# Part of the last gate's weights loaded early, on GpSimd's DMA queue, onto chosen partitions

## The chip, the cores and the metric

One core of a Trainium2 chip runs one decode step of a transformer block for four sequences. The metric is device time in microseconds (us), the median of several runs. The core has five engines with a queue each: TensorE (PE, whose weight loads the profile lists as PEld), VectorE (DVE), ScalarE (ACT), GpSimd (POOL) and SyncE (SP). All loads from HBM go through 16 DMA engines, which the queues of SP, ACT and GpSimd feed.

## What is computed

The reference, cut to what matters:

```python
mod = (silu(c) @ w_mod).reshape(4, 6, 1, -1)          # c: 4x512, w_mod: 512x3072
sa, ca, ga, sb, cb, gb = (mod[:, i] for i in range(6))
h = layernorm(x) * (1 + ca) + sa
x = x + ga * attention(h, last 2048 keys and values of 8192, wq, wo)
h = layernorm(x) * (1 + cb) + sb
x = x + gb * ((silu(h @ w1) * (h @ w3)) @ w2)          # w1, w3: 512x1792, w2: 1792x512
```

The last gate, gb, is `silu(c)` (4x512) times the last 512 columns of `w_mod`: 512 weight rows of 512 numbers, 1 MiB in float32. Keys, values and weights together are 101.2 MB, and nothing is read twice.

## The kernel before

Everything is float32. The sequence of loads is written out by hand on SP's queue (`load`, L88 to L125), in the order in which the data are used: the tile `T0` with `c` and two parts of `w_mod`, then for each of eight key/value heads 8 MB into one of two big buffers `KV[0]`, `KV[1]`, with the attention weights `wq`, `wo` (tile `WP`) between them, then the weights of the other gates (`wm_in`), of w1 and w3 (`f1_in`, `f2_in`), of gb (`gb_in`, L123), and at last w2 in six pieces (`W2_CUTS`, L124 and L125). ACT's queue takes the first `WP` load and x. SP waits before a load until the buffer's last reader is done (`x_done`, `a_done`, `qt_done`), and otherwise issues ahead. GpSimd only fills a few tiles at the start (L128 to L139) and passes semaphores on.

`sc` (L188) is silu(c), transposed: 128 partitions by 4 chunks by 4 sequences. PE forms the first modulations from it at the start (L303), and SP's load of the second head waits for them (L95). After the attention loop come, on PE: the modulations ga, sb, cb (L381, into bank bX), the transposes of the normalized h (L405), the products with w1 and w3 (L416 to L432), the transposes of u (L447), the gate gb (L454: four matmuls, one for each chunk of 128 weight rows, into four bands of 32 partitions of bank bM, that a later product with `same` adds up, L474), and the products with w2 (L462 to L485), each piece after its own load. VectorE multiplies by the gate (L488), adds x (L490), and SP stores the result (L492).

Matmuls are recorded in the helper `mm`, so in the profile all of them have its line, L255; loads by SP have L89 and transposes in `turn` L276.

Of the kernel before, what the change touches and what calls it, by code (L numbers as in the profile page):

```python
# [5 lines left out]
AF = mybir.ActivationFunctionType  # L6
# [4 lines left out]
B, D, HQ, G, SK, DH, W, FF = 4, 512, 32, 8, 8192, 128, 2048, 1792  # L11
P = 128
# [2 lines left out]
EPS = 1e-5  # L15
CHUNKS = [(j, c) for c in range(4) for j in range(4) if c < 2 or j < 3]
HEAD = 8
W2_CUTS = [0, 4, 8, 10, 12, 13, 14]
PAIRS = G // 2

# [20 lines left out]
        return (self.sem, self.n)  # L41


def block_kernel(nc, x_in, t0_in, t1_in, kv_in, w_in, wm_in, f1_in, f2_in, gb_in, w2_in, out):
    T, v, s, gp, S = nc.tensor, nc.vector, nc.scalar, nc.gpsimd, nc.sync

    def sems(names):
        return [nc.alloc_semaphore(n) for n in names.split()]

    def sb(name, cols, rows=P):  # L50
        return nc.alloc_sbuf_tensor(name, (rows, cols), F32).ap()

    def bank(name):
        return nc.alloc_psum_tensor(name, (P, 512), F32).ap()

    (first,) = sems("first")
    A = Queue(nc, s, "act")
    V = Queue(nc, v, "dve")
    L = Queue(nc, gp, "pool")
    dx, dt0, dt1, dkv, dk, dva, dvb, dwo, dm, df1, df2a, df2b, dgb = sems("dx dt0 dt1 dkv dk dva dvb dwo dm df1 df2a df2b dgb")  # L60
    dw = sems(" ".join(f"dw{i}" for i in range(len(W2_CUTS) - 1)))
    z_ok, q_ok, p_ok, k_ok, va_ok, vb_ok, pt_ok, o_ok, ot_ok = sems("z_ok q_ok p_ok k_ok va_ok vb_ok pt_ok o_ok ot_ok")
    s_done, q_done, qt_done, pp_done, o_done, x_done, a_done, pe, last = sems("s_done q_done qt_done pp_done o_done x_done a_done pe last")
# [1 line left out]

    KV = [sb("KV0", 16384), sb("KV1", 16384)]
    WP = sb("WP", 8192)
    T0 = KV[1][:, : 16 + 4096]
    x_sb = sb("x_sb", 512, B)
    ident, same, eps = sb("ident", P), sb("same", B), sb("eps", 1)  # L70
    sc, e1, e2 = sb("sc", 16), sb("e1", 16), sb("e2", 16)
    hT, h2T = sb("hT", 16), sb("h2T", 16)
    Z = sb("Z", B * 28)
    q_sb, p_sb, o_sb, a_sb, y_sb, g_sb, u_sb, gb_sb = [sb(n, 512) for n in "q_sb p_sb o_sb a_sb y_sb g_sb u_sb gb_sb".split()]
# [10 lines left out]
    bS, bQ, bT, bP, bO, bX, bA, bM = [bank(n) for n in "bS bQ bT bP bO bX bA bM".split()]  # L85


    def load(dst, src, sem):  # L88
        S.dma_start(dst, src).then_inc(sem, 16)  # L89

    load(T0, t0_in, dt0)
    s.dma_start(WP[:, 4096:], t1_in).then_inc(dt1, 16)
# [27 lines left out]
    S.wait_ge(x_done, G)  # L120
    load(KV[1][:, :3072], f2_in[:, :3072], df2a)
    load(KV[1][:, 3072:6144], f2_in[:, 3072:], df2b)
    load(KV[1][:, 6144:8192], gb_in, dgb)  # L123
    for a, b, sem in zip(W2_CUTS[:-1], W2_CUTS[1:], dw):  # L124
        load(KV[1][:, 8192 + a * 512 : 8192 + b * 512], w2_in[:, a * 512 : b * 512], sem)  # L125


    l_eps = L.op(gp.memset(eps, EPS))  # L128
    t = L.op(gp.memset(ident, 0.0))
    L.wait(t)  # L130
# [48 lines left out]
    v_same = V.op(v.tensor_reduce(same, ident.rearrange("p (j i) -> p i j", i=32)[:, :B, :], axis=AX.X, op=ALU.add))  # L179

    A.wait((dt0, 16))
    t = A.op(s.activation(e1, T0[:, :16], AF.Exp, scale=-1.0))
    V.wait(t)
    t = V.op(v.tensor_scalar(e2, e1, 1.0, None, op0=ALU.add))
    V.wait(t)
    t = V.op(v.reciprocal(e2, e2))
    V.wait(t, (dt0, 16))
    t_sc = V.op(v.tensor_mul(sc, T0[:, :16], e2))  # L188

    A.wait((pe, 1))  # L190
    t_sa = A.op(s.copy(sa_sb, bM[32 : 32 + B, :]))
# [1 line left out]
    t = V.op(v.scalar_tensor_tensor(xs, bM[:B, :], 1.0, xc, op0=ALU.add, op1=ALU.mult))  # L193
# [60 lines left out]
    def mm(o, lhsT, rhs, start=True, stop=True):  # L254
        return T.matmul(o, lhsT, rhs, start=start, stop=stop, skip_group_check=True)  # L255
# [46 lines left out]
    T.wait_ge(V.sem, t_sc[1])  # L302
    for k in range(4):  # L303
        for i in range(2):
            ins = mm(bM[32 * i : 32 * i + B, :], sc[:, k * B : (k + 1) * B], T0[:, 16 + (2 * k + i) * 512 : 16 + (2 * k + i + 1) * 512], k == 0, k == 3)
    ins.then_inc(pe, 1)
    T.wait_ge(V.sem, t_h[1])
    for k in range(4):
        ins = T.transpose(bT[:, k * B : (k + 1) * B], h[:, k * P : (k + 1) * P], ident[:B, :B])
# [71 lines left out]
    for k in range(4):  # L381
        for i in range(3):
            at = (3 * k + i) * 512
            ins = mm(bX[32 * i : 32 * i + B, :], sc[:, k * B : (k + 1) * B], KV[0][:, at : at + 512], k == 0, k == 3)
# [3 lines left out]

    V.wait((pe, 3), t_ga)
    t = V.op(v.tensor_mul(ag, bM[:B, :], ga_sb))  # L390
    V.wait(t)
    t_x1 = V.op(v.scalar_tensor_tensor(x1, ag, 1.0, x_sb, op0=ALU.mult, op1=ALU.add, accum_out=st2[:, 0:1]))
    t_ss, t_r0, t_xc = stats(x1, t_x1, st2)
# [10 lines left out]
    for k in range(4):  # L404
        ins = T.transpose(bT[:, k * B : (k + 1) * B], h[:, k * P : (k + 1) * P], ident[:B, :B])  # L405
# [4 lines left out]
    def view(t_):  # L410
        return t_.rearrange("p (c j i) -> p c j i", c=4, j=4)
# [4 lines left out]
    for k in range(4):  # L416
        for j in range(4):
            at = 6144 + k * 2048 + j * 512
            ins = mm(bQ[32 * j : 32 * j + B, :], h2T[:, k * B : (k + 1) * B], KV[0][:, at : at + 512], k == 0, k == 3)
# [3 lines left out]
    for k in range(4):  # L423
# [5 lines left out]
        for j in range(3):  # L429
            at = k * 1536 + j * 512  # L430
            ins = mm(bA[32 * j : 32 * j + B, :], h2T[:, k * B : (k + 1) * B], KV[1][:, at : at + 512], k == 0, k == 3)
    ins.then_inc(pe, 1)  # L432
    A.wait((pe, 7))
    t = A.op(s.activation(view(eT), view(bP)[:, :, :, :B], AF.Exp, scale=-1.0))
    V.wait(t)
    t = V.op(v.tensor_scalar(dT, eT, 1.0, None, op0=ALU.add))
    V.wait(t)
    t = V.op(v.reciprocal(rT, dT))
# [7 lines left out]
    for c in range(4):  # L446
        ins = T.transpose(bS[:, c * P : c * P + 96], u_sb[:96, c * P : (c + 1) * P], ident[:96, :96])  # L447
# [3 lines left out]


    T.wait_ge(dgb, 16)
    for k in range(4):  # L454
        ins = mm(bM[32 * k : 32 * k + B, :], sc[:, k * B : (k + 1) * B], KV[1][:, 6144 + 512 * k : 6144 + 512 * (k + 1)])
    ins.then_inc(pe, 1)
    A.wait((pe, 10))
    t_gb = A.op(s.copy(gb_sb, bM))
    T.wait_ge(V.sem, t_hid[1])
    hw = view(hidT)  # L460
    w2 = KV[1][:, 8192 : 8192 + 14 * 512].rearrange("p (n m) -> p n m", n=14)
    for i in range(len(W2_CUTS) - 1):  # L462
        T.wait_ge(dw[i], 16)
        for n in range(W2_CUTS[i], W2_CUTS[i + 1]):
            jj, c = CHUNKS[n]
            if n < HEAD:
                ins = mm(bO[32 * (n % 4) : 32 * (n % 4) + B, :], hw[:, c, jj, :], w2[:, n, :], n < 4, n >= HEAD - 4)
                continue
            for j in range(4):
                ins = mm(bX[32 * j : 32 * j + B, :P], hw[:, c, jj, :], w2[:, n, j * P : (j + 1) * P], n == HEAD, n == 13)  # L470
        if i == 0:
            T.wait_ge(A.sem, t_gb[1])
            for j in range(4):
                ins = mm(bT[32 * j : 32 * j + B, :P], same, gb_sb[:, j * P : (j + 1) * P])  # L474
# [13 lines left out]
    t = V.op(v.tensor_mul(yt, bX[:, :P], gbJ))  # L488
# [8 lines left out]
def _layout(i):  # L497
    import numpy as np

    def a(t):  # L500
        return np.ascontiguousarray(t)

    k = i["A_k_cache"][:, :, SK - W :, :].reshape(B, G, NT, 512, DH)
    v = i["A_v_cache"][:, :, SK - W :, :].reshape(B, G, NT, 4, P, DH)
    k = k.transpose(1, 4, 2, 0, 3).reshape(G, P, 8192)
    v = v.transpose(1, 4, 2, 0, 3, 5).reshape(G, P, 8192)
    wm = i["w_mod"].reshape(4, P, 6, 512).transpose(1, 0, 2, 3)
    c = i["c"].reshape(B, 4, P).transpose(2, 1, 0).reshape(P, 16)
    wq = i["A_wq"].reshape(4, P, G, 512).transpose(2, 1, 0, 3).reshape(G, P, 2048)
    wo = i["A_wo"].reshape(G, R, P, D).transpose(0, 2, 1, 3).reshape(G, P, 2048)  # L510
    pairs = [[wo[2 * p], wo[2 * p + 1]] + ([wq[2 * p + 2], wq[2 * p + 3]] if p < 3 else [wo[6], wo[7]]) for p in range(4)]
    w1 = i["B_w1"].reshape(4, P, FF).transpose(1, 0, 2)
    w3 = i["B_w3"].reshape(4, P, FF).transpose(1, 0, 2)
    w2 = i["B_w2"].reshape(14, P, D)
    return {
        "x_in": a(i["A_x"].reshape(B, D)),
        "t0_in": np.concatenate([c, wm[:, :, 1::-1].reshape(P, 4096)], 1),
        "t1_in": np.concatenate([wq[0], wq[1]], 1),
        "kv_in": np.concatenate([k, v], 2),
        "w_in": np.stack([np.concatenate(p, 1) for p in pairs]),  # L520
        "wm_in": a(wm[:, :, 2:5]).reshape(P, 6144),
        "f1_in": np.concatenate([w1, w3[:, :, 1536:]], 2).reshape(P, 8192),
        "f2_in": a(w3[:, :, :1536]).reshape(P, 6144),
        "gb_in": a(wm[:, :, 5]).reshape(P, 2048),
        "w2_in": a(np.stack([w2[4 * j + c_] for j, c_ in CHUNKS], 1)).reshape(P, 14 * D),
    }

# [14 lines left out]
```

## Time and profile before

| | us |
|---|---|
| median of 3 runs | 243.21 (242.92 to 243.47) |
| the profiled execution | 243.12 |
| its span, first to last instruction | 241.8 |
| PE, DVE, ACT busy | 136.2, 38.6, 25.1 |
| read from HBM | 101.20 MB, 419 GB/s over the span |

The profile gives one execution. Its time beyond the span, 1.3 us, is start and end around the instructions. "DMA share" is the mean busy share of the 16 DMA engines in a stretch; it can pass 1.00 in a short one, because a packet counts where it begins. "Instruction" packets of the queues q8 and q14 bring program code to the engines; q1 is SP's queue and q10 ACT's. A DMA's packets are one for each row of a partition, and a packet of 4 bytes on every engine that took part, which counts up the semaphore.

### The profile page before, as it was taken

The page shows a single profiled execution, that of the slowest core. Times are in us where ns is not written, and L with a number is a line of the kernel's source. Part 1 is how long each engine was busy: PE and PEld are TensorE (multiplying, and loading weights), DVE is VectorE, ACT ScalarE, POOL GpSimd, SP SyncE. Part 2 cuts the span into 40 slices and gives each one's busy share as a digit, 9 for nine tenths or more (in the row PEclk, how much of TensorE's full clock was granted, in tenths as well). Part 3 has the DMA queues.
Part 4 walks back from the last instruction along what each step waited for, and adds up shares of the span by engine and source line. Part 5 has one row for each costly group of instructions (what it writes and reads, how often), then busy time and mean ns, then how long its engine had stood idle before and what let it go on. Part 6 is the DMA issues. An engine that isn't in the chain of part 4 may idle for free. (4 is left out here: it accounts for less than half of the span.)

```text
span 241.8 us, 2271 instructions
## 1 busy us (share of the span) xinstructions
PE 136.2 (56%) x940; PEld 37.3 (15%) x940; DVE 38.6 (16%) x126; ACT 25.1 (10%) x54; POOL 1.7 (1%) x14
## 2 busy tenths in 40 slices
PE   3004677817660387276723772667237768665964
PEld 0000121201210012112200121112001222111211
DVE  3003202202200022022000220220002222124122
ACT  2002002100120002001100020001001201123110
POOL 2000000000000000000000000000000000000000
PEclk9999959967996579987985798879858997995999
DMA  7998989899989898999898989998989999999992
GB/s 266 451 500 369 499 371 488 379 417 445 493 379 488 369 499 381 407 428 510 369 499 369 499 369 423 434 510 369 499 350 442 442 400 440 453 431 396 418 411 106
DMA packets 4044, 101.33 MB, mean 419 GB/s; under 512 B 452, under 2 KB 580, under 8 KB 1096
## 3 DMA queue, kind: packets, MB, share of 16 engines
q1 hardware_dynamic: 3888, 99.17, 95.6%
q10 hardware_dynamic: 152, 2.11, 2.1%
q8 instruction: 3, 0.05, 0.1%
q14 instruction: 1, 0.01, 0.0%
HBM read 101.20 MB, written 0.07 MB: 419 GB/s over the span
## 5 line engine op out<-in xcount | busy, mean ns | idle before, releaser
L255 PE MATMUL bS<-KV,Z 128*16 128x512 f32 x256 | 42.5, 824 | 38.8 <-PEq L258 38.8
L255 PE MATMUL bO<-KV,pT 128*16 128x512 f32 x256 | 31.9, 642 | 0.5
L255 PEld LDWEIGHTS bS<-KV,Z 128*16 128x16 f32 x256 | 9.1, 122 | 66.6 <-issue 66.6
L218 DVE TENSOR_REDUCE MX<-bS 128x1 f32<-128x512 f32 x8 | 5.5, 691 | 79.6 <-PE bS L255 79.6
L255 PE MATMUL bM<-KV,sc 128*4 128x512 f32 x24 | 7.3, 835 | 16.6 <-DVE sc L188 16.6
L367 ACT ACTIVATE p_sb<-bS,NB 128x512 f32<-128x512 f32 x8 | 5.5, 687 | 101.2 <-ACTq L358 101.2
L276 PE MATMUL bP<-ident,p_sb 128*128 128x128 f32 x32 | 5.0, 280 | 17.3 <-PEq L258 17.3
L255 PE MATMUL bA<-WP,oT 128*4 128x512 f32 x64 | 10.4, 728 | 5.2 <-PEq L258 5.2
L255 PEld LDWEIGHTS bO<-KV,pT 128*16 128x16 f32 x256 | 8.1, 105 | 22.9 <-issue 22.9
L372 ACT ACTIVATE o_sb<-bO,LB 128x512 f32<-128x512 f32 x8 | 5.5, 687 | 48.7 <-ACTq L358 48.7
L255 PE MATMUL bQ<-WP,hT 128*4 128x512 f32 x64 | 9.2, 648 | 0.6 <-DVE hT L197 0.6
L276 PE MATMUL bX<-ident,o_sb 128*128 128x128 f32 x32 | 5.0, 280 | 7.9 <-PEq L258 7.9
L244 DVE TENSOR_REDUCE oT<-bX 128x16 f32<-128x64 f32 x8 | 1.8, 224 | 44.0 <-PE bX L276 44.0
L276 PE MATMUL bT<-ident,q_sb 128*128 128x128 f32 x32 | 5.5, 298 | 3.6 <-PEq L258 3.6
L276 PEld LDWEIGHTS bP<-ident,p_sb 128*128 128x128 f32 x32 | 3.4, 140 | 24.4 <-issue 24.4
L276 PEld LDWEIGHTS bX<-ident,o_sb 128*128 128x128 f32 x32 | 3.4, 141 | 15.0 <-issue 15.0
L227 DVE COPY pT<-bP 128x256 f32<-128x256 f32 x8 | 3.4, 424 | 13.7 <-PE bP L276 13.7
L255 PE MATMUL bQ<-KV,h2T 128*4 128x512 f32 x32 | 5.3, 831 | 0.3 <-DVE h2T L408 0.3
L276 PEld LDWEIGHTS bT<-ident,q_sb 128*128 128x128 f32 x32 | 3.7, 150 | 8.3 <-issue 8.0
L255 PEld LDWEIGHTS bM<-KV,sc 128*4 128x4 f32 x24 | 1.0, 106 | 22.6 <-DVE sc L188 18.2
L255 PE MATMUL bX<-KV,sc 128*4 128x512 f32 x24 | 4.4, 592 | 0.0
L202 DVE TENSOR_REDUCE Z<-bT 128x16 f32<-128x64 f32 x8 | 1.8, 224 | 15.4 <-PE bT L276 15.1
(101 smaller groups left out, 68.0 us busy)
## 6 DMA issues: line engine op xcount, KB each, us to landing
WP<-w_in SPq DMA_DIRECT2D x3, 4096.0 KB, 18.9
KV<-kv_in SPq DMA_DIRECT2D x1, 4096.0 KB, 24.1
KV<-f_in SPq DMA_DIRECT2D x1, 4096.0 KB, 25.9
KV<-kv_in SPq DMA_DIRECT2D x1, 3072.0 KB, 30.9
KV<-wm_in SPq DMA_DIRECT2D x1, 3072.0 KB, 16.5
KV<-f_in SPq DMA_DIRECT2D x2, 1536.0 KB, 17.2
KV<-t_in SPq DMA_DIRECT2D x1, 2056.0 KB, 12.3
WP<-t_in ACTq DMA_DIRECT2D x1, 2048.0 KB, 12.5
```

What stands on the lines that cost most here:

```text
L202: v.tensor_reduce(Z.rearrange("p (b i) -> p b i", b=B)[:, :, 12 : 12 + R], bT.rearrange("p (r k i) -> p i r k", r=R, k=4)[:, :B], axis=AX. ...
L218: t = V.op(v.reduce_max(MX[:, 0:1], bS, axis=AX.X))
L227: v.tensor_copy(pT.rearrange("p (t b c r) -> p c b t r", t=NT, b=B, c=4), bP.rearrange("p (c b i) -> p c b i", c=4, b=B)[:, :, :, :16].rea ...
L244: V.op(v.tensor_reduce(oT.rearrange("p (r b) -> p r b", r=R), diag, axis=AX.X, op=ALU.add), ot_ok)
L255: return T.matmul(o, lhsT, rhs, start=start, stop=stop, skip_group_check=True)
L276: ins = T.transpose(dst[:, c * P : (c + 1) * P], src[:, c * P : (c + 1) * P], ident)
L367: A.op(s.activation(p_sb, bS, AF.Exp, bias=NB[:, 0:1], accum_out=SM[:, 0:1]), p_ok)
L372: A.op(s.mul(o_sb, bO, LB[:, 0:1]), o_ok)
```

## The change

Of the gate's 512 weight rows, 256 stay as they were: two chunks of 128 rows in `gb_in`. The next 64 rows, 256 to 319, stay in `gb_in` too, with the two halves of each row on two partitions (256 columns more). So `gb_in` has 1280 columns, not 2048. The last 192 rows are loaded at the kernel's start by GpSimd into a tile `GC`, on partitions 0 to 15 (two rows each), 16 to 31 and 64 to 79 (five each). A fourth transfer, into `GZ`, is read by nothing. GpSimd clears `GC` first. The matching entries of c (28 columns) travel with `T0`, so `sc` and its two helpers are 44 columns wide, not 16. PE multiplies `GC` in five matmuls behind the first gate's product and later adds the rest of the gate to them, two matmuls of 512 columns and two of 256.

```diff
+BANDS, SHARE = [0, 16, 64], [2, 5, 5]
+SUB = max(SHARE)
+C_IN = 16 + 4 * SUB + 8
+W2_AT = 6144 + 1280
...
+    GC, GZ = sb("GC", SUB * 512, 80), sb("GZ", 256, 96)
...
-    load(KV[1][:, 6144:8192], gb_in, dgb)
+    load(KV[1][:, 6144:W2_AT], gb_in, dgb)
...
+    t = L.op(gp.memset(GC, 0.0))
+    L.wait(t)
+    gp.dma_start(GC[:16, : SHARE[0] * 512], ga_in[:, :4]).then_inc(dgc, 16)
+    for e, at in enumerate(BANDS[1:]):
+        gp.dma_start(GC[at : at + 16], gc_in[4 * e : 4 * e + 4, :4]).then_inc(dgc, 16)
+    gp.dma_start(GZ[80:], ga_in[:, :4, :256]).then_inc(dgc, 16)
...
     t = V.op(v.tensor_mul(ag, bM[:B, :], ga_sb))
+    T.wait_ge(V.sem, t[1])
+    T.wait_ge(dgc, 64)
+    for m in range(SUB):
+        j = m % 4
+        mm(bM[32 * j : 32 * j + B, :], sc[:80, 16 + m * B : 16 + (m + 1) * B], GC[:, m * 512 : (m + 1) * 512], m < 4, False)
...
-    for k in range(4):
-        ins = mm(bM[32 * k : 32 * k + B, :], sc[:, k * B : (k + 1) * B], KV[1][:, 6144 + 512 * k : 6144 + 512 * (k + 1)])
+    for k in range(2):
+        mm(bM[32 * k : 32 * k + B, :], sc[:, k * B : (k + 1) * B], KV[1][:, 6144 + 512 * k : 6144 + 512 * (k + 1)], False, True)
+    for k in range(2):
+        at = 16 + 4 * SUB + k * B
+        ins = mm(bM[64 + 32 * k : 64 + 32 * k + B, 256 * k : 256 * (k + 1)], sc[:, at : at + B], KV[1][:, 7168:7424], False, True)
...
+    ga, gc = (np.zeros((len(r), 5, r.shape[2]), c.dtype) for r in (rows[0], np.concatenate(rows[1:])))
+    ga[:, :4], gc[:, :4] = rows[0], np.concatenate(rows[1:])
```

In HBM the new arrays have an outer dimension of 4 with 5 rows each, of which 4 are read (`[:, :4]`), so each of the four transfers has a source of 4 by 4 rows. Its 16 rows are of 4 KB (`GC`, first band), 10 KB (the two others) and 1 KB (`GZ`).

GpSimd's queue at the kernel's start, before and after (line numbers are each kernel's own):

```order
L535 MEMSET const-uint8-127 128x1
L128 MEMSET eps 128x1
L129 MEMSET ident 128x128
L132 ISA
L132 AFFINE_SELECT ident<-ident 128x128
L135 MEMSET y_sb 128x512
```

```order
L568 MEMSET const-uint8-127 128x1
L134 MEMSET GC 80x2560 [waits barrier_Pool_Activation_PE_DVE_SP_gather]
L136 DMA GC<-ga_in 16x1x1024 [waits pool]
L138 DMA GC<-gc_in 16x1x2560 x2
L139 DMA GZ<-ga_in 16x1x256
L140 MEMSET eps 128x1
L141 MEMSET ident 128x128
L144 ISA [waits pool]
```

The memset and the four transfers stand ahead of `eps` and `ident`, which were first.

PE's queue behind the attention loop, before and after (bX takes ga, sb, cb; bT the transposes of h; bQ the products with w1):

```order
L255 MATMUL bM<-a_sb,same 4x512 [waits dve]
L354 UNCONDITIONAL_BRANCH
L255 MATMUL bX<-KV,sc 4x512 [waits dm]
L255 MATMUL bX<-KV,sc 4x512 x11
L405 MATMUL bT<-ident,h 128x4 [waits dve]
L405 MATMUL bT<-ident,h 128x4 x3
L255 MATMUL bQ<-KV,h2T 4x512 [waits df1,dve]
```

```order
L267 MATMUL bM<-a_sb,same 4x512 [waits dve]
L366 UNCONDITIONAL_BRANCH
L267 MATMUL bX<-KV,sc 4x512 [waits dm]
L267 MATMUL bX<-KV,sc 4x512 x11
L267 MATMUL bM<-GC,sc 4x512 [waits dgc,dve]
L267 MATMUL bM<-GC,sc 4x512 x4
L422 MATMUL bT<-ident,h 128x4 [waits dve]
L422 MATMUL bT<-ident,h 128x4 x3
```

The five matmuls on `GC` now stand between bX and the transposes of h, with a wait for VectorE's product `ag`, the last reader of bM.

PE's queue at the gate, before and after (bS takes the transposes of u, bO the first products with w2):

```order
L447 MATMUL bS<-ident,u_sb 128x96 [waits dve]
L447 MATMUL bS<-ident,u_sb 128x96 x3
L255 MATMUL bM<-KV,sc 4x512 [waits dgb]
L255 MATMUL bM<-KV,sc 4x512 x3
L255 MATMUL bO<-KV,hidT 4x512 [waits dw0,dve]
```

```order
L464 MATMUL bS<-ident,u_sb 128x96 [waits dve]
L464 MATMUL bS<-ident,u_sb 128x96 x3
L267 MATMUL bM<-KV,sc 4x512 [waits dgb]
L267 MATMUL bM<-KV,sc 4x512
L267 MATMUL bM<-KV,sc 4x256 x2
L267 MATMUL bO<-KV,hidT 4x512 [waits dw0,dve]
```

Two of the gate's four matmuls here are half as wide; the place is the same.

## Rows read from the trace of the kernel before

**Rows 1.** The page's 40 slices: busy tenths of the DMA engines, and GB/s

```profile
DMA  7998989899989898999898989998989999999992
GB/s 266 451 500 369 499 371 488 379 417 445 493 379 488 369 499 381 407 428 510 369 499 369 499 369 423 434 510 369 499 350 442 442 400 440 453 431 396 418 411 106
```

**Rows 2.** Windows, steady: stretch, us, busy PE/PEld/DVE/ACT/POOL, clock, DMA share, GB/s

```profile
36.00:208.00 172.00, 100.55 (x709) 28.60 (x702) 24.29 (x86) 15.46 (x31) 0.00 (x0) 0.83 1.00 432
226.00:230.00 4.00, 4.00 (x36) 1.01 (x25) 0.89 (x3) 0.81 (x2) 0.00 (x0) 1.00 1.00 417
230.00:235.00 5.00, 3.36 (x34) 0.82 (x28) 1.14 (x4) 0.85 (x2) 0.00 (x0) 1.00 1.00 412
```

**Rows 3.** The chain that ended last: start, us, what

```profile
211.81 0.43 SPq L89
...
212.29 26.78 DMA KV<-w_in
...
239.11 0.45 PE bX L255 x8
```

**Rows 4.** The same windows over the last microseconds of the load stream

```profile
237.00:237.25 0.25, 0.25 (x16) 0.07 (x8) 0.12 (x1) 0.00 (x0) 0.00 (x0) 1.00 0.37 139
237.30:237.90 0.60, 0.31 (x12) 0.04 (x8) 0.00 (x0) 0.00 (x0) 0.00 (x0) 1.00 0.20 75
...
237.60:238.00 0.40, 0.13 (x8) 0.13 (x12) 0.00 (x0) 0.00 (x0) 0.00 (x0) 1.00 0.17 67
...
238.05:238.60 0.55, 0.55 (x21) 0.25 (x16) 0.00 (x0) 0.00 (x0) 0.00 (x0) 1.00 0.13 52
...
238.40:238.70 0.30, 0.30 (x12) 0.11 (x8) 0.00 (x0) 0.00 (x0) 0.00 (x0) 1.00 0.09 34
238.70:241.00 2.30, 0.59 (x16) 0.11 (x8) 0.58 (x2) 0.00 (x0) 0.00 (x0) 1.00 0.00 0
```

**Rows 5.** DMA queues from 32 to 36 us: packets, MB, share of 16 engines

```profile
q8 instruction: 1, 0.02, 1.6%
```

**Rows 6.** DMA queues from 93 to 96 us

```profile
q14 instruction: 1, 0.01, 0.7%
```

**Rows 7.** DMA queues from 212 to 216 us

```profile
q8 instruction: 1, 0.02, 1.7%
```

**Rows 8.** DMA queues from 236.9 to 237.0 us

```profile
q8 instruction: 1, 0.02, 68.7%
```

**Rows 9.** The page's DMA issues: size in KB, us from issue to landing

```profile
KV<-gb_in SPq DMA_DIRECT2D x1, 1024.0 KB, 20.8
```

**Rows 10.** The page's DMA queues of SP and ACT: packets, MB, share

```profile
q1 hardware_dynamic: 3888, 99.17, 95.6%
q10 hardware_dynamic: 152, 2.11, 2.1%
```

**Rows 11.** Timeline of the start: start, us, engine, what, [idle before <-releaser]

```profile
1.43 0.52 POOL L135 MEMSET y_sb<- 128x512 f32 x1
...
19.58 0.29 ACT L156 ACTIVATE st<-st,eps 4x1 f32<-4x1 f32 x1
...
21.25 6.27 PE L255 MATMUL bM<-KV,sc 128*4 128x512 f32 x16 [16.65 <-DVE sc L188]
```

**Rows 12.** Windows: the stretch after SP's first wait has ended

```profile
28.00:32.00 4.00, 2.29 (x12) 0.43 (x12) 1.17 (x3) 0.15 (x1) 0.00 (x0) 0.76 1.21 524
```

**Rows 13.** Timeline behind the loop, PE and DVE

```profile
216.03 0.68 DVE L390 TENSOR_TENSOR ag<-bM,ga_sb 4x512 f32<-4x512 f32 x1 [5.26 <-ACT ga_sb L387]
...
220.26 0.58 PE L405 MATMUL bT<-ident,h 4*128 4x4 f32 x4 [4.98 <-DVE h L398]
...
228.09 0.42 PEld L276 LDWEIGHTS bP<-ident,g_sb 128*128 128x128 f32 x4 [0.86 <-DMA KV<-f_in]
...
235.32 1.04 PE L255 MATMUL bO<-KV,hidT 128*4 128x512 f32 x8 [1.16 <-DMA KV<-w_in]
```

More of the change, by code (lines that the diff above doesn't have):

```diff
@@ L41, in op, with block_kernel @@
         return (self.sem, self.n)
-def block_kernel(nc, x_in, t0_in, t1_in, kv_in, w_in, wm_in, f1_in, f2_in, gb_in, w2_in, out):
+def block_kernel(nc, x_in, t0_in, t1_in, kv_in, w_in, wm_in, f1_in, f2_in, gb_in, ga_in, gc_in, w2_in, out):
     T, v, s, gp, S = nc.tensor, nc.vector, nc.scalar, nc.gpsimd, nc.sync
@@ L59, in block_kernel @@
     L = Queue(nc, gp, "pool")
-    dx, dt0, dt1, dkv, dk, dva, dvb, dwo, dm, df1, df2a, df2b, dgb = sems("dx dt0 dt1 dkv dk dva dvb dwo dm df1 df2a df2b dgb")
+    dx, dt0, dt1, dkv, dk, dva, dvb, dwo, dm, df1, df2a, df2b, dgb, dgc = sems("dx dt0 dt1 dkv dk dva dvb dwo dm df1 df2a df2b dgb dgc")
     dw = sems(" ".join(f"dw{i}" for i in range(len(W2_CUTS) - 1)))
@@ L67, in block_kernel @@
     WP = sb("WP", 8192)
-    T0 = KV[1][:, : 16 + 4096]
+    GC, GZ = sb("GC", SUB * 512, 80), sb("GZ", 256, 96)
+    T0 = KV[1][:, : C_IN + 4096]
     x_sb = sb("x_sb", 512, B)
     ident, same, eps = sb("ident", P), sb("same", B), sb("eps", 1)
-    sc, e1, e2 = sb("sc", 16), sb("e1", 16), sb("e2", 16)
+    sc, e1, e2 = sb("sc", C_IN), sb("e1", C_IN), sb("e2", C_IN)
     hT, h2T = sb("hT", 16), sb("h2T", 16)
@@ L122, in block_kernel @@
     load(KV[1][:, 3072:6144], f2_in[:, 3072:], df2b)
-    load(KV[1][:, 6144:8192], gb_in, dgb)
+    load(KV[1][:, 6144:W2_AT], gb_in, dgb)
     for a, b, sem in zip(W2_CUTS[:-1], W2_CUTS[1:], dw):
-        load(KV[1][:, 8192 + a * 512 : 8192 + b * 512], w2_in[:, a * 512 : b * 512], sem)
+        load(KV[1][:, W2_AT + a * 512 : W2_AT + b * 512], w2_in[:, a * 512 : b * 512], sem)
+    t = L.op(gp.memset(GC, 0.0))
[4 more added lines that the diff above has]
+    gp.dma_start(GZ[80:], ga_in[:, :4, :256]).then_inc(dgc, 16)
     l_eps = L.op(gp.memset(eps, EPS))
@@ L181, in block_kernel @@
     A.wait((dt0, 16))
-    t = A.op(s.activation(e1, T0[:, :16], AF.Exp, scale=-1.0))
+    t = A.op(s.activation(e1, T0[:, :C_IN], AF.Exp, scale=-1.0))
     V.wait(t)
@@ L187, in block_kernel @@
     V.wait(t, (dt0, 16))
-    t_sc = V.op(v.tensor_mul(sc, T0[:, :16], e2))
+    t_sc = V.op(v.tensor_mul(sc, T0[:, :C_IN], e2))
     A.wait((pe, 1))
@@ L304, in block_kernel @@
         for i in range(2):
-            ins = mm(bM[32 * i : 32 * i + B, :], sc[:, k * B : (k + 1) * B], T0[:, 16 + (2 * k + i) * 512 : 16 + (2 * k + i + 1) * 512], k == 0, k == 3)
+            ins = mm(bM[32 * i : 32 * i + B, :], sc[:, k * B : (k + 1) * B], T0[:, C_IN + (2 * k + i) * 512 : C_IN + (2 * k + i + 1) * 512], k == 0, k == 3)
     ins.then_inc(pe, 1)
@@ L460, in block_kernel @@
     hw = view(hidT)
-    w2 = KV[1][:, 8192 : 8192 + 14 * 512].rearrange("p (n m) -> p n m", n=14)
+    w2 = KV[1][:, W2_AT : W2_AT + 14 * 512].rearrange("p (n m) -> p n m", n=14)
     for i in range(len(W2_CUTS) - 1):
@@ L508, in _layout @@
     c = i["c"].reshape(B, 4, P).transpose(2, 1, 0).reshape(P, 16)
+    ct, w5 = i["c"].reshape(B, 512).T, i["w_mod"][:, 5 * 512 :]
+    cs = np.zeros((P, 4 * SUB + 8), c.dtype)
+    rows, at = [], 320
+    for p, n in zip(BANDS, SHARE):
+        cs[p : p + 16, : 4 * n] = ct[at : at + 16 * n].reshape(n, 16, B).transpose(1, 0, 2).reshape(16, 4 * n)
+        rows.append(w5[at : at + 16 * n].reshape(n, 16, 512).transpose(1, 0, 2).reshape(4, 4, n * 512))
+        at += 16 * n
+    cs[:64, 4 * SUB : 4 * SUB + 4], cs[64:, 4 * SUB + 4 :] = ct[256:320], ct[256:320]
+    ga, gc = (np.zeros((len(r), 5, r.shape[2]), c.dtype) for r in (rows[0], np.concatenate(rows[1:])))
+    ga[:, :4], gc[:, :4] = rows[0], np.concatenate(rows[1:])
+    half = w5[256:320].reshape(64, 2, 256).transpose(1, 0, 2).reshape(P, 256)
     wq = i["A_wq"].reshape(4, P, G, 512).transpose(2, 1, 0, 3).reshape(G, P, 2048)
@@ L516, in _layout @@
         "x_in": a(i["A_x"].reshape(B, D)),
-        "t0_in": np.concatenate([c, wm[:, :, 1::-1].reshape(P, 4096)], 1),
+        "t0_in": np.concatenate([c, cs, wm[:, :, 1::-1].reshape(P, 4096)], 1),
         "t1_in": np.concatenate([wq[0], wq[1]], 1),
@@ L523, in _layout @@
         "f2_in": a(w3[:, :, :1536]).reshape(P, 6144),
-        "gb_in": a(wm[:, :, 5]).reshape(P, 2048),
+        "gb_in": np.concatenate([a(wm[:, :2, 5]).reshape(P, 1024), half], 1),
+        "ga_in": ga,
+        "gc_in": gc,
         "w2_in": a(np.stack([w2[4 * j + c_] for j, c_ in CHUNKS], 1)).reshape(P, 14 * D),
```

## The prediction

> **What bounds the kernel now.** I read the page's slices first. The DMA row stands at 7 to 9 tenths in every slice but the last [rows 1], and the windows show a share of 1.00 from 36 to 208 us and again from 226 to 235 us [rows 2]. The 16 DMA engines are thus full from the first microseconds to the end of the stream, while PE is busy for 136.2 of 241.8 us. The chain confirms it: its last long piece is the final load of w2, which lands at 212.29 + 26.78 = 239.07 us, and PE has 0.45 us of work behind it [rows 3]. So the time is the time of the load stream, and every byte that is added anywhere costs, however early, as long as it runs on the DMA engines that end last.
>
> The last windows show how unevenly the stream ends [rows 4]. Share times 16 is the number of engines at work. From 238.05 to 238.60 the share is 0.13, two engines; from 237.30 to 237.90 it is 0.20, three. The ends follow from the areas. From 238.40 to 238.70, 0.09 x 0.30 x 16 = 0.43 engine-us, so the two stop 0.22 us in, at 238.62. From 237.60 to 238.00, 0.17 x 0.40 x 16 = 1.09, of which the two use 0.80; the third stops at 237.89. From 237.00 to 237.25, 0.37 x 0.25 x 16 = 1.48, of which the three use 0.75; the other 13 have 0.73 left, so on average they stop at 237.06 and the last of them about 237.25. The late two are about 1.4 us behind the last of the others, the third 0.6. From 237.00 on, 1.48 + 0.15 + 1.92 + 0.30 + 1.14 + 0.04 = 5.03 engine-us are left; spread over 16 engines they would end at 237.31. No rearrangement of the load gains more than 238.62 - 237.31 = 1.3 us.
>
> Where the lag is from is an inference. Packets of program code run on the same engines: one of 16 KB between 32 and 36 us, one of 8 KB between 93 and 96, one of 16 KB between 212 and 216 [rows 5 to 7]. Two large and one half as large fit two engines 1.4 us late and one 0.6 late. As records they last 1.6% x 4 us x 16 = 1.0 us and 0.7% x 3 x 16 = 0.34. A fourth packet, of 16 KB, begins after 236.9, when most engines have nothing left; it lasts 68.7% x 0.1 x 16 = 1.1 us [rows 8], and no fourth engine is late.
>
> **The change, part by part.** *Removed from the tail.* The gate's load is 1024 KB on SP's queue [rows 9] and becomes 640: 384 KB less, 24 KB on each engine. An engine moves 412/16 = 25.8 GB/s in the stretch with rows of 8 KB, 432/16 = 27.0 in the long one [rows 2]. I take 25.8 throughout, as the new rows are of 10 KB and less: 24,576 B are 0.95 us for every engine.
>
> *Added to all.* 28 columns of c are 112 B on each of 128 partitions, 896 B an engine: 0.03 us.
>
> *Added at the start, and on which engines?* This decides. ACT's queue carried two DMAs, the 128 rows of WP and the 4 rows of x, and has 152 packets [rows 10]: 128 + 16 semaphore packets for the first and 4 + 4 for the second. SP's count bears this reading out: 27 DMAs of 128 + 16 are 3888. So a transfer whose outer dimension is 4 runs on 4 engines. All four new ones have 4 there: 4 rows an engine, which makes 16 KB in the first, 40 KB in the next two, 4 KB in the unread one. No row shows which four engines each takes. If each takes another four, every engine is in one of these classes; with 0.64, 1.59, 1.59 and 0.16 us for the new bytes the net per engine is
>
> - 16 KB: -0.95 + 0.03 + 0.64 = -0.28
> - 40 KB (eight engines): -0.95 + 0.03 + 1.59 = +0.67
> - 4 KB: -0.95 + 0.03 + 0.16 = -0.76
>
> [...]
>
> I take it that the late two are among the four with 4 KB, and the third in the 16 KB class: the shares 2, 5, 5 and almost nothing fit lags of 0.6, none, none and 1.4. Ends after: the late two 238.62 - 0.76 = 237.86, the third 237.89 - 0.28 = 237.61, the 40 KB engines at worst 237.25 + 0.67 = 237.92, on average 237.06 + 0.67 = 237.73. So the stream ends at 237.86 to 237.92, **0.70 to 0.76 us earlier**.
>
> *What hides the rest.* GpSimd's memset of 2560 columns is five times the 0.52 us of the 512-column one, 2.6 us, and four issues follow; `eps` must be there by 19.58, when ACT first reads it [rows 11], so each issue may take 3.6 us at no cost, against 0.43 for SP's [rows 3]. Were the whole opening later, SP's second head load would be issued later; but the first one still fills the engines from 28 to 32 us [rows 12], so 4 us are free. PE's five matmuls are ten passes; at the start 16 passes took 6.27 us [rows 11], so at most 3.9. They may begin at 216.71, and the transposes of h wait until 220.26 [rows 13]: 3.5 us of cover. The 0.4 us that could stick out end in the 0.86 us for which PE waits on f2 [rows 13]. f2 itself comes up to 0.25 us later, since all the new bytes precede it: the late two gain 0.19 and the 40 KB engines, 1.4 ahead, 1.62. PE still waits 1.16 us for w2's second piece [rows 13], so with that piece 0.7 earlier there is 0.4 left. No compute takes the loads' place.
>
> Sum against the profiled execution: 243.12 - 0.70 = 242.42. That execution is 0.09 under the median of 243.21, so I forecast **242.5**.
>
> **Rivals.** *Heavy shares on late engines (slower).* If four engines are picked otherwise and a late one gets 40 KB, it ends at 238.62 + 0.67 = 239.29: 243.21 + 0.67 = 243.9. It decides as soon as one of the late two is among the eight. For it: no row ties an engine to a transfer, and eight of 16 is a wide target. Against it: the fit of the shares above.
>
> *The fourth code packet comes earlier (no change).* PE's program gets five matmuls and two waits ahead of the tail. If the packet at 236.9 brings PE's code and comes at a fixed place in it, it moves to a time when its engine still has 2 us to load, and costs the 1.4 us that the others cost. That engine had ended by about 236.9. In the 40 KB class it would end at 236.9 + 0.67 + 1.4 = 238.97, 0.35 later than now: 243.6. In the 16 KB class it would be 236.9 - 0.28 + 1.4 = 238.0, a time of 242.6; in the last class nothing. For it: the added code. Against: one class in two hurts.
>
> *It doesn't do what it says (no change).* If GpSimd's transfers spread over all 16 engines, each gets 400/16 = 25 KB back, 0.99 us: -0.95 + 0.03 + 0.99 = +0.07, a time of 243.3. [...] The share of 0.13 at the end [rows 4] speaks against it: the engines are shared, but not evenly loaded, and bytes can still be dealt out anew.
>
> *Only part of the gain.* One late engine spared and the other in the 16 KB class: 238.62 - 0.28, a time of 242.9.
>
> **Chances.** Forecast 0.53; heavy shares on late engines 0.17; early code packet 0.12 at 243.6; even spread 0.10; part of the gain 0.08. A measurement of this kernel can tell about 0.2%, 0.49 us, from no change: faster means under 242.72, slower over 243.70. So faster 0.53, within 0.2% 0.30, slower 0.17. The range leaves out the slower rival: up to 243.6; below the forecast it goes to 242.2, for the gain of 0.76, the 0.09 of the median and runs that differ by 0.3. It holds 0.83.
>
> **What would show it.** Right: the windows from 237.3 on empty in one step, with no stretch of two or three busy engines (0.13 to 0.20); the last w2 load lands near 238.4; GpSimd's queue has 64 packets with data, four transfers of 16 rows; w2's pieces land about 0.7 us earlier and f2 at most 0.25 later. Wrong: a share of 0.06 or 0.13 that lasts to 239 (a late engine got a heavy share, or the code packet moved), a code packet before 236, or PE without a wait before w2's pieces.

## The result: two kinds of time, and the longer one is the median

| | median of 20 runs, us | all runs |
|---|---|---|
| before | 243.08 | 242.84 to 243.47 |
| after | 243.70 | 242.44 to 243.99 |

The ratio after to before is 1.0018, with a 95% interval of 1.0010 to 1.0026: 0.18% slower, which by the prediction's measure is within 0.2%. The median hides what happened. The times after are of two kinds with a gap between them: 4 of 20 lie from 242.44 to 242.83, as forecast, and 16 from 243.48 to 243.99. Nothing of the kind is seen before. The profiled execution is of the shorter kind, at 242.60, so its trace shows the change as it was meant, and it says nothing on the longer kind.

The chain of waits of the kernel after, which answers to [rows 3] (start, us, what):

```profile
210.88 27.65 DMA KV<-w_in
...
238.57 0.45 PE bX L267 x8
```

The last load of w2 lands at 238.53, not 239.07: 0.54 us earlier. The windows over the last microseconds answer to [rows 4] (stretch, length, busy time of PE, PEld, DVE, ACT, POOL, granted clock, DMA share, GB/s):

```profile
237.00:237.25 0.25, 0.05 (x4) 0.00 (x0) 0.00 (x0) 0.00 (x0) 0.00 (x0) 1.00 0.79 303
237.30:237.90 0.60, 0.56 (x16) 0.32 (x16) 0.00 (x0) 0.00 (x0) 0.00 (x0) 1.00 0.41 154
237.60:238.00 0.40, 0.40 (x20) 0.12 (x12) 0.00 (x0) 0.00 (x0) 0.00 (x0) 1.00 0.19 72
238.05:238.60 0.55, 0.34 (x12) 0.04 (x11) 0.00 (x0) 0.00 (x0) 0.00 (x0) 1.00 0.00 0
```

Before, three engines worked from 237.30 to 237.90 and two until 238.62. Now most still work up to 237.25 (0.79 x 16 = 13), and from 238.05 to 238.60 the share is 0.00, at 0 GB/s. The stretch in which two engines worked alone until 238.62 is gone; the engines still end one after the other, with three at work on average from 237.60 to 238.00 (0.19 x 16 = 3.0), and not in the one step that was forecast.

GpSimd's part, from the DMA queues (packets, MB, share), the DMA issues (KB each, us from issue to landing) and the timeline (start, us):

```profile
q0 software_dynamic: 272, 0.41, 0.5%
...
GC<-gc_in POOLq DMA_DIRECT2D x2, 160.0 KB, 26.7
...
GC<-ga_in POOLq DMA_DIRECT2D x1, 64.0 KB, 10.6
...
GZ<-ga_in POOLq DMA_DIRECT2D x1, 16.0 KB, 35.8
```

```profile
0.73 2.23 POOL L134 MEMSET GC<- 80x2560 f32 x1 [0.29 <-POOLq L568]
...
3.27 0.69 POOL L136 DMA_DIRECT2D GC<-ga_in  x1 [0.31 <-POOL GC L134]
3.96 1.10 POOL L138 DMA_DIRECT2D GC<-gc_in  x2
5.05 0.57 POOL L139 DMA_DIRECT2D GZ<-ga_in  x1
5.60 0.12 POOL L140 MEMSET eps<- 128x1 f32 x1
...
216.18 1.88 PE L267 MATMUL bM<-GC,sc 80*4 80x512 f32 x10 [1.47 <-DVE ag L402]
...
219.68 0.43 PE L422 MATMUL bT<-ident,h 4*128 4x4 f32 x4 [1.62 <-DVE h L415]
```

The memset takes 2.2 us, an issue 0.55 to 0.7; `eps` is set at 5.7, 14 us before ACT needs it. The queue's 0.41 MB are the 400 KB of the four transfers; its 272 packets are not the 64 rows and 16 semaphore packets that four engines a transfer would have by the prediction's way of counting, so on this queue the count doesn't tell how many engines took part. The transfers land late, beside SP's stream, the last 36 us after its issue; PE wants them at 216. Its ten passes end at 218.06, before the transposes of h at 219.68. What the prediction called hidden is hidden.

### The profile page after: what moved, and what is told of

The parts are those of the page before. It is cut to its first block, busy times and chain, and to the rows that moved or that the text cites. A ratio compares the mean times of both kernels' runs of the same rounds, so it can differ in the third digit from the quotient of the medians.

```text
span 241.3 us, 2297 instructions
## 1 busy us (share of the span) xinstructions
PE 139.0 (58%) x950; PEld 38.0 (16%) x950; DVE 38.9 (16%) x126; ACT 25.1 (10%) x54; POOL 6.3 (3%) x19
## 5 line engine op out<-in xcount | busy, mean ns | idle before, releaser
L267 PE MATMUL bS<-KV,Z 128*16 128x512 f32 x256 | 43.8, 846 | 39.6 <-PEq L270 39.6
L267 PE MATMUL bO<-KV,pT 128*16 128x512 f32 x256 | 31.3, 632 | 0.5
L288 PE MATMUL bP<-ident,p_sb 128*128 128x128 f32 x32 | 6.3, 333 | 17.3 <-PEq L270 17.3
L267 PE MATMUL bM<-KV,sc 128*4 128x512 f32 (+1 forms) x24 | 6.1, 691 | 12.8 <-DVE sc L200 12.8
L267 PE MATMUL bA<-WP,oT 128*4 128x512 f32 x64 | 10.9, 759 | 1.8 <-PEq L270 1.8
L267 PE MATMUL bQ<-WP,hT 128*4 128x512 f32 x64 | 8.3, 592 | 0.6 <-DVE hT L209 0.6
L288 PEld LDWEIGHTS bP<-ident,p_sb 128*128 128x128 f32 x32 | 4.2, 166 | 24.7 <-issue 24.7
L267 PE MATMUL bQ<-KV,h2T 128*4 128x512 f32 x32 | 6.5, 982 | 0.8 <-DMA KV<-f_in 0.8
L267 PE MATMUL bA<-y_sb 128*128 128x512 f32 x2 | 2.1, 1141 | 7.4 <-POOL x1J L151 7.4
L267 PE MATMUL bX<-KV,sc 128*4 128x512 f32 x24 | 3.6, 592 | 0.7 <-DMA KV<-wm_in 0.7
```

The costliest lines, as they stand in the source:

```text
L288: ins = T.transpose(dst[:, c * P : (c + 1) * P], src[:, c * P : (c + 1) * P], ident)
```

## The experiments

Two theories stood first: that in the longer executions the heavy shares lie on late engines, or that the packet of program code near the end comes earlier and makes one more engine late.

**The changed kernel again**, unaltered, beside two others.

> The changed kernel once more. Its executions took two kinds of time, 242.4 to 242.8 us (4 of 20) and 243.5 to 244.0 us (16 of 20), and the one profiled so far was of the first kind, with the late two engines gone. Theory 'dealt otherwise': in the longer executions the heavy shares lie on the late engines, 0.67 us added to 238.6: two kinds of time again, and a trace of the longer kind ends with a few engines over 1 us behind the others. Rival 'code packet': the packet of program code that began at 236.5 in the profiled execution comes earlier in the longer ones and holds up one engine by 1.4 us: the trace then ends with a single engine (share 0.06) and the packet before 235.

Measured 242.59 (242.47 to 242.74, 4 runs) against 243.19, ratio 0.9975 (0.9961 to 0.9989). Only the shorter kind. Neither theory is touched.

**Without the fourth transfer:**

```diff
-    gp.dma_start(GZ[80:], ga_in[:, :4, :256]).then_inc(dgc, 16)
...
-    T.wait_ge(dgc, 64)
+    T.wait_ge(dgc, 48)
```

> The changed kernel without the fourth, unread transfer, whose data nothing needs. 'Dealt otherwise': if each transfer takes the four engines behind those of the one before, and this goes on from one execution to the next, three transfers shift the deal by 12 engines each time: four kinds of time in turn, about 242.5, 243.2, 243.8 and 243.8 us. If the deal starts anew each time, there is one kind, the same as with the fourth. 'Code packet': the fourth transfer makes no difference, the two kinds stay as they were.

Measured 242.44 (242.32 to 242.59, 4 runs) in the same comparison, ratio 0.9969 (0.9955 to 0.9983). One kind in four runs, so these times show nothing that shifts from one execution to the next, and the fourth transfer gives nothing (242.59 with it).

**Code without transfers**, all four of them taken away and the whole gate loaded by SP again:

```diff
-W2_AT = 6144 + 1280
+W2_AT = 6144 + 2048
...
-    gp.dma_start(GC[:16, : SHARE[0] * 512], ga_in[:, :4]).then_inc(dgc, 16)
...
-    gp.dma_start(GZ[80:], ga_in[:, :4, :256]).then_inc(dgc, 16)
...
+    for k in range(4):
+        ins = mm(bM[32 * k : 32 * k + B, :], sc[:, k * B : (k + 1) * B], KV[1][:, 6144 + 512 * k : 6144 + 512 * (k + 1)], False, True)
```

> All four transfers of GpSimd left out, and the whole gate loaded by SP as in the kernel before; the memset of GC, the 28 more columns of c and the five matmuls (which add zeros) stay. 'Dealt otherwise': the kernel before plus 0.03 us for the columns, 243.1, one kind of time. 'Code packet': PE's code is as long as in the changed kernel, so the longer executions appear here too, 0.4 to 1.4 us above the kernel before in most of them.

Measured 243.37 (243.08 to 243.41), ratio 1.0004 (0.9990 to 1.0019): no gain without the transfers, and no second kind 0.4 us or more above, in four runs. The window shows the late engines where they were before, 0.17 x 16 = 2.7 of them by their busy time and two by the rate, which is the 52 GB/s of [rows 4]:

```profile
238.05:238.60 0.55, 0.52 (x20) 0.23 (x16) 0.00 (x0) 0.00 (x0) 0.00 (x0) 1.00 0.17 52
```

**A second occasion, the order of the transfers, and an even spread.**

> The changed kernel on another occasion, beside the next two. In the last comparison all its executions were of the shorter kind (242.47 to 242.74) and two engines no longer ended late; of the 20 behind the result 16 were of the longer kind (243.5 to 244.0). Theory 'dealt otherwise': which four engines the first transfer gets is set by something outside the kernel that differs between occasions; if this occasion gives the longer kind, the trace ends with two to four engines over 1 us behind. If all are 242.6 again, nothing new.

Measured 242.64 (242.49 to 242.82, 4 runs): the shorter kind alone again.

```diff
+    gp.dma_start(GZ[80:], ga_in[:, :4, :256]).then_inc(dgc, 16)
     gp.dma_start(GC[:16, : SHARE[0] * 512], ga_in[:, :4]).then_inc(dgc, 16)
...
-    gp.dma_start(GZ[80:], ga_in[:, :4, :256]).then_inc(dgc, 16)
```

> The unread transfer issued first of the four, all else as in the changed kernel: the same bytes, each class of engines moved on by four. 'Dealt otherwise': where the changed kernel is at 242.6, here the late two are in a 40 KB class, 238.62 + 0.67 = 239.3 in place of 237.9, a time of 243.8 to 243.9, and the last windows show two engines (0.13) for over 1 us. Rival 'order does not matter' (the engines are shared evenly or chosen anew each time): the same time as the changed kernel, within 0.1.

Measured 248.44 (248.38 to 248.61), ratio 1.0216 (1.0202 to 1.0231). The order matters, but at 5.8 us above the changed kernel, not the 1.2 expected: something else is at work, which the last windows don't show. The packets and the rate of the DMA queues from 12 to 45 us do, first after, then here:

```profile
DMA packets 488, 14.52 MB, mean 440 GB/s; under 512 B 226, under 2 KB 226, under 8 KB 237
```

```profile
DMA packets 463, 12.75 MB, mean 386 GB/s; under 512 B 222, under 2 KB 222, under 8 KB 237
```

(440 - 386) / 440 x 33 us = 4.1 us are lost while GpSimd's transfers run.

```diff
-    load(KV[1][:, 6144:8192], gb_in, dgb)
+    load(KV[1][:, 6144:7424], gb_in, dgb)
...
+    gp.dma_start(GE, ge_in).then_inc(dge, 16)
```

> 384 KB of the gate's load go to GpSimd's queue at the kernel's start too, but as 768 columns of all 128 partitions in one transfer, so on all 16 engines alike; PE multiplies them at the place of the five matmuls. 'Dealt otherwise': only the deal among the engines gives time, so this is the kernel before within 0.1, 243.1 to 243.3, and ends with the same two late engines. Rival: loading early, outside SP's stream, is what gains: 242.4 to 242.6.

Measured 243.12 (242.96 to 243.27), ratio 0.9996 (0.9982 to 1.0011). Here, against the kernel before, one transfer fills 128 partitions of 768 columns. The same 384 KB on the same queue at the same time, but over all partitions, which I take to be on all engines alike, bring nothing (243.19 before), and the late two are back (48 GB/s, 52 before):

```profile
238.05:238.60 0.55, 0.55 (x16) 0.26 (x16) 0.00 (x0) 0.00 (x0) 0.00 (x0) 1.00 0.13 48
```

So the gain of the shorter kind, at 242.5 to 242.8 in the same comparison, is in how the bytes are dealt, not in the early load. This is what the prediction's rival "it doesn't do what it says" would be, at its price of 243.3 within 0.2.

**The changed kernel alone in turn with the kernel before.**

> The changed kernel alone in turn with the kernel before, as behind the result, on a third occasion. On two occasions beside other kernels it was at 242.5 to 242.8 in all eight runs. If the longer kind (243.5 to 244.0, 16 of the 20 runs behind the result) comes from what runs between its executions, it shows up here in most of them, and its trace tells whether two late engines, one held-up engine or a general loss is behind it. If it is 242.6 throughout, the kind hangs on the occasion (the chip), not on the order of the runs.

Measured 243.71 (242.59 to 243.98, 12 runs; four below 243.0, eight from 243.57 up), ratio 1.0016 (1.0004 to 1.0028). Both kinds again. To catch the longer one in a trace:

> The changed kernel, unaltered, to get a trace of its longer kind (243.5 to 244.0 us), which the third occasion showed again in 8 of 12 runs; all traces so far are of the shorter kind. Theory 'code packets move': the two 16 KB code packets fall on other engines in the longer executions; one that falls in a 40 KB class ends at 237.92 + 1.4 = 239.3, a time of 243.8, and the last windows show one or two engines for over 1 us. Rival 'deal moves': GpSimd's transfers take other engines; then, as with the unread transfer first, the loss is general and near 5 us, not 1.2.

> The same kernel, unaltered, the second of the call: a trace of the longer kind is wanted. The two theories expect what stands with the first.

> The same kernel, unaltered, the third of the call: a trace of the longer kind is wanted. The two theories expect what stands with the first.

Measured 242.66, 242.63 and 242.43: three more of the shorter kind. All seven traces of the changed kernel are of it.

**Where are the late two?** The unread transfer third, on partitions 64 to 79, and the last 80 weight rows fourth, on 80 to 95:

```diff
-BANDS, SHARE = [0, 16, 64], [2, 5, 5]
+BANDS, SHARE = [0, 16, 80], [2, 5, 5]
...
-    for e, at in enumerate(BANDS[1:]):
-        gp.dma_start(GC[at : at + 16], gc_in[4 * e : 4 * e + 4, :4]).then_inc(dgc, 16)
-    gp.dma_start(GZ[80:], ga_in[:, :4, :256]).then_inc(dgc, 16)
+    gp.dma_start(GC[16:32], gc_in[:4, :4]).then_inc(dgc, 16)
+    gp.dma_start(GZ[64:], ga_in[:, :4, :256]).then_inc(dgc, 16)
+    gp.dma_start(GC[80:], gc_in[4:, :4]).then_inc(dgc, 16)
```

> The unread transfer third, not fourth, and the last 80 weight rows on partitions 80 to 95 in place of 64 to 79: the third four engines get 4 KB, the last four 40 KB; the first two classes and what partitions belong to which transfer's place in the order stay. If the late two are among the last four (the prediction's step), both now get 40 KB: 238.62 + 0.67 = 239.29, a time of 243.8, the longer kind made on purpose; the last windows show two engines for 1.4 us. If a general loss as with the unread transfer first (248.4) comes from the order alone, 248 again.

Measured 244.03, 244.06, 243.91, 243.96 and, in the fifth run, 242.69; ratio 1.0027 (1.0005 to 1.0049). The trace, of the first run, is as expected, two engines alone up to 239.45, and the last load lands at 214.82 + 25.04 = 239.86:

```profile
238.05:238.60 0.55, 0.35 (x8) 0.06 (x8) 0.00 (x0) 0.00 (x0) 0.00 (x0) 1.00 0.14 52
238.60:239.20 0.60, 0.56 (x16) 0.32 (x16) 0.00 (x0) 0.00 (x0) 0.00 (x0) 1.00 0.12 48
239.20:239.45 0.25, 0.23 (x12) 0.11 (x8) 0.00 (x0) 0.00 (x0) 0.00 (x0) 1.00 0.11 41
239.45:240.00 0.55, 0.32 (x12) 0.09 (x8) 0.00 (x0) 0.00 (x0) 0.00 (x0) 1.00 0.00 0
```

In this execution, as in the traced ones of the changed kernel, that fits late engines among those of the last transfer, which are four by the prediction's estimate: with 160 KB in that transfer the time is of the longer kind, 244.03, with 16 KB 242.60. The fifth run, at 242.69, says that this is not so in every execution.

**The same order and bytes, other partitions:**

```diff
-BANDS, SHARE = [0, 16, 64], [2, 5, 5]
+BANDS, SHARE = [16, 64, 0], [2, 5, 5]
...
-    gp.dma_start(GC[:16, : SHARE[0] * 512], ga_in[:, :4]).then_inc(dgc, 16)
+    gp.dma_start(GC[16:32, : SHARE[0] * 512], ga_in[:, :4]).then_inc(dgc, 16)
```

> The three parts of GC on other partitions, 16 to 31 (two rows each), 64 to 79 and 0 to 15 (five each); order, bytes and engines of the four transfers as in the changed kernel. If only the bytes of each engine count, 242.6, no change. If the loss of 5 us with the unread transfer first came from engines that write to partitions which other engines write to in SP's stream, the same loss shows here: 246 to 249 us, spread over all the stream from 12 to 45 us.

Measured 248.00 (246.63 to 248.62), ratio 1.0214 (1.0197 to 1.0231). With order and bytes unchanged, the partitions alone cost 5 us against the 242.6 of the shorter kind. The unread transfer first leaves each part on its partitions and changes only the order, so its loss is most likely the same, by my estimate. What the two have in common is the pairing of order and partitions: all kernels here whose four transfers go to partitions 0, 16, 64 and 80 in that order took 242.4 to 244.2 us, and these two, which go to 16, 64, 0 and 80 and to 80, 0, 16 and 64, took 246.6 to 248.6. No row names the engines of a transfer: that the transfers take four after four in their order was an estimate. Why the other pairings cost time no row shows.

**What varies?** Three explanations of the longer kind were left: the late engines change from execution to execution; the deal shifts from one to the next; repeated executions pay for GpSimd's transfers wherever they lie.

> The kernel with the unread transfer third, alone in turn with the kernel before. With it the late two got 40 KB in four of five runs (243.9 to 244.1); the fifth took 242.69. Theory 'the late engines change': in some executions the code packets hold up engines of other classes; those that make the changed kernel long (a late one in the 40 KB classes) can make this one short, so both kinds appear here too, 242.5 to 243.0 and 243.5 to 244.1, and nothing above. Rival 'repeated executions pay 1.2 us for GpSimd's transfers, wherever they lie': here the first kind is 244.0 and the longer one 245.2; 242.69 was a stray.

Measured 243.98 (243.88 to 244.16, 5 runs): no run above 244.2, which speaks against a fixed price on top of the heavy share. The short kind did not come back; over both comparisons it is one run of ten.

> The changed kernel without the unread transfer, alone in turn with the kernel before, as the changed kernel was on the third occasion, where it took two kinds of time. Three transfers of four engines leave a running deal 12 engines further on. Theory 'the late engines change': the deal starts anew with each execution, so the fourth transfer is idle; two kinds as in the changed kernel, about 0.1 shorter: 242.4 to 242.8 and 243.4 to 243.9, none at 248. Rival 'the deal shifts': if it runs on from one execution to the next, three of four executions have their bytes on engines that do not fit the partitions, and take 246 to 249 us, as in the runs with the unread transfer first and with other partitions.

Measured 243.62 (242.48 to 243.90, 12 runs), three from 242.48 to 242.76 and nine from 243.43 up, ratio 1.0014 (1.0004 to 1.0024). Two kinds as with the fourth transfer, and nothing near 248, where by the expectation's estimate a deal that shifts by 12 engines would have put three executions of four. The times speak against such a shift.

**Does program code make engines late?** 64 more matmuls on PE at the start of the kernel before:

```diff
     T.wait_ge(L.sem, l_z[1])
+    for _ in range(64):
+        mm(bA[:, :4], zero[:, :P], zero[:, :4])
```

> The kernel before with 64 more matmuls of 4 columns on PE, in the first microseconds, in which PE waits (they write zeros that the next matmul writes again). They lengthen PE's code by 256 instructions or more and load nothing from HBM but code. If packets of program code are what makes engines late, there are one or two more of 16 KB in the stream and one or two more late engines: the share from 238.05 to 238.60 goes from 0.13 to 0.19 or 0.25, at the same time of 243.1 where all fall on different engines (up to 244.6 if one engine gets two). If the lateness has another cause, the share stays 0.13.

Measured 250.35 (250.22 to 250.52) against 243.07: they took 29 us, and PE's first products with `sc`, for which SP's load of the second head waits, began at 31.84, not 21.25. It can't answer.

```profile
2.53 29.38 PE L255 MATMUL bA<-y_sb 128*128 128x4 f32 x130 [2.53 <-POOL x1J L139]
```

With `zero[:4, :4]` on both sides:

> The kernel before with 64 more matmuls on PE in its first microseconds, of 4 rows and 4 columns, so that they end before PE is wanted at 21 us (in the first form they took 29 us, and the stream ran dry for it). PE's code is 256 instructions longer or more, and nothing else is loaded. If packets of program code make engines late, one or two more packets of 16 KB make one or two more engines late: the share from 238.05 to 238.60 goes from 0.13 to 0.19 or 0.25 at the same time of 243.1 (up to 244.6 if one engine gets two). If the lateness has another cause, it stays 0.13.

Measured 243.19, beside 243.24 before, one run of each. The extra matmuls end at 7.9 us. There is one more packet of code (q8, four in place of three) and one more late engine, 0.18 x 16 = 2.9 in place of 2. The share alone would not show it, since `code_only` has 0.17 with three packets; the rate does, 71 GB/s in place of 52 there and before and of 48 in `even`:

```profile
q8 instruction: 4, 0.07, 0.1%
```

```profile
238.05:238.60 0.55, 0.54 (x20) 0.25 (x16) 0.00 (x0) 0.00 (x0) 0.00 (x0) 1.00 0.18 71
```

So one more packet of program code, between 7 and 11 us, went with one more late engine at the end, in the one trace that there is.

**Which class holds the late engine of the longer kind?** The small share in the second transfer, then in the third (with bands [64, 0, 16]), the partitions in the same order as in the changed kernel:

```diff
-BANDS, SHARE = [0, 16, 64], [2, 5, 5]
+BANDS, SHARE = [16, 0, 64], [2, 5, 5]
...
+    gp.dma_start(GC[:16], gc_in[:4, :4]).then_inc(dgc, 16)
+    gp.dma_start(GC[16:32, : SHARE[0] * 512], ga_in[:, :4]).then_inc(dgc, 16)
+    gp.dma_start(GC[64:], gc_in[4:, :4]).then_inc(dgc, 16)
```

> The first and second transfer exchange their sizes: the first four engines get 40 KB, the second four 16, the third four 40, the last four 4, each on its own partitions. Alone in turn with the kernel before. The third late engine (0.6 us), if it is among the first four as the prediction took it, now sets the end: 237.89 + 0.67 = 238.56, 243.1. Theory 'the late engines change': in the executions that are long with the changed kernel, a late one is in the second or third class. If in the second, it gets 16 KB here, 238.62 - 0.28 = 238.34: no long kind, 243.1 in all. If in the third, two kinds, 243.1 and 243.6 to 244.0.

Measured 243.35 (242.96 to 243.86, 11 runs): five from 242.96 to 243.15, one of 243.35, five from 243.64 up; ratio 1.0017 (1.0007 to 1.0026).

> The first and third transfer exchange their sizes: the first and second four engines get 40 KB, the third four 16, the last four 4, each on its own partitions. Alone in turn with the kernel before. In the shorter executions 243.1 again, by the third late engine in the first class. If the late engine of the longer executions is in the third class, it gets 16 KB here, 238.34: no long kind. If it is in the second, two kinds, 243.1 and 243.6 to 244.0.

Measured 243.29 (243.05 to 243.80, 11 runs): eight from 243.05 to 243.40, three from 243.62 up; ratio 1.0012 (1.0003 to 1.0021). The longer kind stays with either, so, by the prediction's estimate of the classes, no one class holds its late engine. No version gains in all of its comparisons.

The lower times are near the 243.1 that the third late engine in the first class was to give. The traces don't bear that reason out. That of `third_light` is of a run of 243.29; that of `second_light` is of a run of 243.71, and so shows an execution of that kernel's longer kind. First `second_light`, then `third_light`:

```profile
238.05:238.60 0.55, 0.28 (x12) 0.28 (x16) 0.00 (x0) 0.00 (x0) 0.00 (x0) 1.00 0.20 78
...
238.70:241.00 2.30, 1.04 (x27) 0.22 (x16) 0.58 (x2) 0.00 (x0) 0.00 (x0) 1.00 0.01 4
```

```profile
238.05:238.60 0.55, 0.55 (x16) 0.26 (x16) 0.00 (x0) 0.00 (x0) 0.00 (x0) 1.00 0.20 75
```

If the late two were among the last four, with 4 KB in both kernels, the third late engine would work alone until 238.56 by the table of ends, and an engine held up by an early code packet at most beside it, until 238.97. Three do (0.20 x 16, at 78 and 75 GB/s). With `second_light` one goes on: 0.01 x 2.30 x 16 = 0.4 engine-us are left after 238.70, and the last load lands at 213.62 + 25.90 = 239.52, 1.0 us later than in the changed kernel's trace. A late engine with 40 KB was to end at 238.62 + 0.67 = 239.29; this one ends at 239.52 - 0.45 = 239.07. So in these two executions the late engines are not all where the prediction put them; which they are, no row tells.

## Why the prediction was wrong, step by step

- **What bounds the kernel, and the uneven end.** Right: `even` shows that the early load over all partitions leaves the late engines and the time as they were (48 GB/s at the end and 243.12, where 52 and 243.19 were before). That packets of code make engines late had been an inference; `more_code2` fits it, in one trace, with one packet more and 71 GB/s in place of 52.
- **The sum.** Nearly right for the kind of execution that it was made for: 242.42 from the profiled execution, 242.5 forecast and 242.60 in the trace. The last load lands at 238.53 where 237.92 and 0.45 more, as before (239.07 - 238.62), give 238.37, so the stream gained 0.54 us of the 0.70. Three other comparisons gave 242.4 to 242.8 in all 11 runs.
- **What hides the rest, and four engines for each transfer.** The first was right, by the timeline above. The second is not shown on GpSimd's queue, where 272 packets don't tell it; the times of `third_unread` and `even` agree with it.
- **The step that failed** is "I take it that the late two are among the four with 4 KB". It fits the seven traces of the changed kernel, where the last load lands at 238.32 to 238.67, and that of `third_unread`, and was taken for a property of the kernel. In 16 of the 20 executions behind the result it doesn't give the time, which is 243.5 to 244.0, and the traces of `second_light` and `third_light` don't fit it. What the runs show in its place is a time of two kinds, with the longer one near the 243.9 that the prediction put on 40 KB on a late engine; why the longer one comes stays open. The table of ends rested on one execution of the kernel before, whose time can't show which engines are late: by the prediction's sums they were equally loaded, so any two give 243.1.
- **The rivals.** Heavy shares on late engines was priced at 243.9, an early code packet at 243.6; the longer kind is at 243.5 to 244.0. The prices fit, the chances (0.29 together) were too low if one of the two is the cause. The early packet as I argued it, moved by 2 us by the added matmuls, is not in the trace: the packet begins in the window from 236.5 to 237.0, where before it began after 236.9. In executions without a trace it is not excluded. And I priced a wrong deal at +0.7 us in all: with the parts on other partitions, or the order changed, it costs 5 to 6.
- **The range** ended at 243.6, 0.1 below the median. It left out the rival whose price fits the longer kind best.

What stays open is what differs between the executions. That the late engines change fits the two kinds, their distance (about 1.1 us, where the prediction's ends give 239.29 - 237.92 = 1.4), the one short run with `third_unread` and the trace of `second_light`; it is argued, not shown. That the deal shifts by 12 engines without the fourth transfer, or that each repetition pays a fixed price, the times speak against. But no trace of the changed kernel's longer kind was had, and on two occasions beside other kernels all eight runs were of the shorter kind, while alone in turn with the kernel before 4 of 20 and 4 of 12 were. What of that order matters wasn't found. The traces may not stand for the other runs either: in the three comparisons alone with two kinds of time (behind the result, `again3`, `no_fourth_alone`) the profiled run was short each time, at 242.60, 242.84 and 242.58, and of the 41 others 8 were; by chance that has odds of 4/20 x 4/12 x 3/12 = 1 in 60.

## What to carry to other kernels

Where one load stream sets the time, read the DMA share of its last microseconds times 16, and the rate beside it: here 0.13 and 52 GB/s meant two late engines of 16, and early bytes over all partitions gained nothing against that (243.12 against 243.19). Bytes dealt by hand to few partitions gave 242.44 to 242.83 in some executions and 243.48 to 243.99 in others, against 243.08 before, and one trace of the kernel before could not tell that; time the changed kernel many times, and look for two kinds of time, before its median is believed. When bytes are dealt so, try their partitions too: here other partitions for the same bytes cost 5 us (248.0 against 242.6).

## What had not been expected of the hardware

- The same four transfers, 400 KB in 101 MB, cost 5 us or more on other partitions (248.0) or in another order (248.4) against 242.6; with the other order the rate from 12 to 45 us was 386 in place of 440 GB/s.
- One more packet of 16 KB of program code, between 7 and 11 us after the start, went with one more DMA engine late at the end of the stream, over 220 us later (71 in place of 52 GB/s from 238.05 to 238.60; one trace).
- A 64 KB transfer from GpSimd's queue took 10.6 us to land and a 16 KB one 35.8, beside SP's stream.
